# One block's k shift moved from TensorE to ScalarE, VectorE and DMA, with merged rotations, small statistics on ScalarE and a new plan

## The chip, the cores and the metric

The kernel runs on one core of a Trainium2 chip. The metric is the device time of one execution in microseconds. A run is an execution of one kernel; runs are taken in rounds together with runs of the kernel before on the same chip. A ratio is the mean time of one kernel's runs over that of the kernel before in the same rounds, so it isn't quite the ratio of the medians that are quoted; the bracket behind it is its 95% interval. Different jobs ran on different chips, so kernels of different jobs are compared through their ratios. 0.1% is 0.35 us.

## The reference

Two kinds of block alternate, twice each, over 2048 rows of 512 columns:

```python
def _A_ref(q, k, v, shift_k, ssm_k, ssm_D):
    # k_shift: causal sum of 4 taps along the rows, one set of taps per column
    for t in range(4):
        k_shift = k_shift + k_pad[:, t:t + S, :] * shift_k[:, 3 - t][None, None, :]
    kv = k_shift * v
    y  = (causal convolution of kv with ssm_k along the rows, by FFT)   # cut
    return q * (y + kv * ssm_D)

def _B_ref(x, w_gate, w_up, w_down):
    return (silu(x @ w_gate) * (x @ w_up)) @ w_down

x = A_q
for _ in range(2):                      # written out in the reference
    x = x + _A_ref(_layernorm(x), A_k, A_v, A_shift_k, A_ssm_k, A_ssm_D)
    x = x + _B_ref(_layernorm(x), B_w_gate, B_w_up, B_w_down)
```

The products kv don't depend on x, so the convolution is computed once and used by both layers.

## The kernel before

The rows are cut into four blocks of 512, and each block of each layer into two feed-forward units of 256 rows. So there are 16 units, run in the order layer 0 and then layer 1 of block 0, the same of block 1, and so on. TensorE works through the units; the convolution of the next blocks (transforms as matmuls, butterflies and products of spectra on VectorE) is laid between them.

In the profile PE is TensorE, PEld its weight loads, DVE VectorE, ACT ScalarE, POOL GpSimd and SP the engine that issues most DMAs. By the names in the program, z is a normalised row block, ptz and zT its transpose (by TensorE in the first unit, by DMA in all later ones), pf the gate and up matmuls, sg their silu, ht the copied up part and then its product with sg, pd the down projection, ps the transforms and the k shift, vt a block of v and then kv.

A planner decides what stands where. Each piece of work is entered with its engine, an estimate of its cost, the buffers that it reads and writes, and for a DMA the time `lat` from issue to landing. A list scheduler then fixes one order for each engine. Its tuning figures are constants at the head of the file:

```python
SLK = 8.59
ST1 = lambda l, c, h: (l, c, h) in {(0, 2, 0), (0, 3, 0), (1, 0, 1)}   # units whose first statistics go to ScalarE
K_ACT = lambda b: b in {3}            # blocks whose k shift does not use TensorE
T0, FLOOR = -8.68, -22.15
DUR = [21.8, 16.2, 25.01, ...]        # cut
STRETCH = {1: {"PE": 1.87, "DVE": 1.47, "ACT": 1.76, "POOL": 1.0, "SP": 341.8}, ...}   # cut
```

Within an engine the order is strict. An instruction that waits holds up all behind it, and a change of any cost or `lat` may give another order everywhere.

The k shift has two forms. With TensorE, four taps are four accumulating matmuls with diagonal matrices, 64 matmuls of 128 columns in a block:

```python
def shift_mul(b, ring, conv, after=(), due=None):
    for r in range(R):
        ...                            # 16 matmuls of 128 columns: kT (shifted by j rows) x dg[j], j = 0..3
        add("ACT", act(D), lambda ...: nc.scalar.copy(out=ks.t[:], in_=ps.t[:]), ...)
        dve(D, lambda ...: nc.vector.tensor_mul(out=vt[b].t[:, r, :], in0=ks.t[:], in1=vt[b].t[:, r, :]), ...)
```

Without TensorE, 16 ScalarE instructions multiply by a tap, three VectorE sums add the four, four DMA transposes turn the result, and two VectorE products multiply by v:

```python
def shift_mul_t(b):
    for j, (t, h) in ((3, (a, 0)), (2, (a, 1)), (1, (c, 0)), (0, (c, 1))):
        for dt in range(KD):
            add("ACT", 0.66, lambda ...: nc.scalar.activation(..., func=ACT.Copy, scale=tapF.t[:, dt, j:j + 1]), ...)
    for t, h in ((a, 1), (c, 0), (c, 1)):
        dve(4 * D, lambda ...: nc.vector.tensor_add(out=a.t[:, 0], in0=a.t[:, 0], in1=t.t[:, h]), ...)
    for r in range(R):
        add("SP", 1.25, lambda r=r: nc.sync.dma_start_transpose(out=ks.t[:, 0, r], in_=a.t[:, 0, r]), ..., lat=4.0)
    ...                                # two VectorE products of 1024 elements with v
```

The butterflies multiply by i, which swaps real and imaginary part, in four instructions of 512 elements:

```python
def rotated(m, i, j, dst, plus, minus, conv):
    for slot, part, op in ((plus, 0, ALU.subtract), (plus, 1, ALU.add), (minus, 0, ALU.add), (minus, 1, ALU.subtract)):
        dve(D, lambda ...: nc.vector.tensor_tensor(out=dst.t[:, slot, part], in0=m.t[:, i, part], in1=m.t[:, j, 1 - part], op=op), ...)
```

Of the kernel before, what the change touches and what calls it, by code (L numbers as in the profile page):

```python
# [9 lines left out]
P = 128  # L10
F32 = mybir.dt.float32
# [3 lines left out]
ALU = mybir.AluOpType  # L15
# [4 lines left out]
SLK = 8.59  # L20
H_DMA = lambda b: b in {2, 3}
ST1 = lambda l, c, h: (l, c, h) in {(0, 2, 0), (0, 3, 0), (1, 0, 1)}
ST2 = lambda l, c, h: (l, c, h) in {(0, 1, 0), (0, 1, 1), (1, 0, 0)}
ASL = 2.32
K_ACT = lambda b: b in {3}
# [3 lines left out]
HSL = 18.8  # L29
Z_ACT = lambda l, c, h: (l, c, h) in {(0, 1, 1), (0, 3, 0), (0, 3, 1), (1, 0, 0), (1, 0, 1), (1, 1, 1), (1, 2, 0), (1, 2, 1)}  # L30
N_ACT = lambda l, c, h: (l, c, h) in {(0, 3, 0), (0, 3, 1), (1, 1, 0), (1, 3, 0)}
Z_DMA = lambda i, j: False
D_DMA = lambda l, c, h: False
X_PE = lambda l, c, h: (l, c, h) in {(0, 1, 0), (0, 1, 1), (1, 3, 1)}
RINGS = {}
T0, FLOOR = -8.68, -22.15
DUR = [21.8, 16.2, 25.01, 22.43, 22.47, 23.48, 19.26, 20.4, 22.2, 24.98, 20.06, 26.08, 20.64, 23.98, 22.98, 26.0]
STRETCH = {1: {"PE": 1.87, "DVE": 1.47, "ACT": 1.76, "POOL": 1.0, "SP": 341.8},
           2: {"PE": 1.0, "DVE": 1.93, "ACT": 1.53, "POOL": 1.0, "SP": 1.62},
           3: {"PE": 1.55, "DVE": 1.54, "ACT": 2.16, "POOL": 1.0, "SP": 2.21}}  # L40
# [231 lines left out]
def kernel(  # L272
# [69 lines left out]
    ident, nhalf = whole("ident", [P, P]), whole("nhalf", [P, 1], F32)  # L342
    tapT, drow = whole("tapT", [P, KD, KS]), new("jk", "drow", [P, D])
# [198 lines left out]
    def rotated(m, i, j, dst, plus, minus, conv):  # L542

        for slot, part, op in ((plus, 0, ALU.subtract), (plus, 1, ALU.add), (minus, 0, ALU.add), (minus, 1, ALU.subtract)):
            dve(D, lambda slot=slot, part=part, op=op: nc.vector.tensor_tensor(
                out=dst.t[:, slot, part], in0=m.t[:, i, part], in1=m.t[:, j, 1 - part], op=op),
                [(m, key((i,), (part,))), (m, key((j,), (1 - part,)))], [(dst, key((slot,), (part,)))], conv=conv)
# [67 lines left out]
    def accumulate(z, sl, slots, part, t):  # L615
        add("POOL", 1.3, lambda: nc.gpsimd.dma_start(out=z.t[:, sl, part, :], in_=t.t[:], accum_op=ALU.add),
            r=[t, (z, key(slots, (part,)))], w=[(z, key(slots, (part,)))], lat=5.0, conv=True)

    def product(i, j, slots=range(4), conv=True):
# [22 lines left out]
        for part in (0, 1):  # L642
            zk = (z, key(slots, (part,)))
            if part and first and Z_DMA(i, j):
                dve(n * D, lambda: nc.vector.tensor_mul(out=z.t[:, sl, 1, :], in0=x.t[:, sl, 0, :], in1=g.t[:, sl, 1, :]),
                    [(x, key(slots, (0,))), (g, key(slots, (1,)))], [zk], conv=conv)
            else:
                t1 = new("t4", "t1", [P, n, D])
                dve(n * D, lambda t1=t1, part=part: nc.vector.tensor_mul(out=t1.t[:], in0=x.t[:, sl, 0, :],  # L649
                                                                         in1=g.t[:, sl, part, :]),  # L650
                    [(x, key(slots, (0,))), (g, key(slots, (part,)))], [t1], conv=conv)
                if part and Z_DMA(i, j):
                    accumulate(z, sl, slots, part, t1)
            t2 = new("t4", "t2", [P, n, D])
            dve(n * D, lambda t2=t2, part=part: nc.vector.tensor_mul(out=t2.t[:], in0=x.t[:, sl, 1, :],  # L655
                                                                     in1=g.t[:, sl, 1 - part, :]),
                [(x, key(slots, (1,))), (g, key(slots, (1 - part,)))], [t2], conv=conv)
            comb = ALU.subtract if part == 0 else ALU.add
            if part and Z_DMA(i, j):
                accumulate(z, sl, slots, part, t2)  # L660
            elif first:
                dve(n * D, lambda t1=t1, t2=t2, part=part, comb=comb: nc.vector.tensor_tensor(
                    out=z.t[:, sl, part, :], in0=t1.t[:], in1=t2.t[:], op=comb), [t1, t2], [zk], conv=conv)
            else:
                dve(n * D, lambda t1=t1, t2=t2, comb=comb: nc.vector.tensor_tensor(  # L665
                    out=t1.t[:], in0=t1.t[:], in1=t2.t[:], op=comb), [t2], [t1], conv=conv)
                if Z_DMA(i, j):
                    accumulate(z, sl, slots, part, t1)
                    continue
                dve(n * D, lambda t1=t1, part=part: nc.vector.tensor_add(  # L670
                    out=z.t[:, sl, part, :], in0=z.t[:, sl, part, :], in1=t1.t[:]), [t1], [zk], conv=conv)
# [57 lines left out]
    def ln_stats_act(c, rows, after=()):  # L729

        n = len(rows)
        mv, sm = new("mv", "mv", [P, n, 2], F32, parts=2 * n), new("st", "sm", [P, 2 * n], F32, parts=2 * n)
        for o, i in enumerate(rows):
            jk = new("jk", "jk", [P, D])
            add("ACT", 0.62, lambda jk=jk, o=o, i=i: nc.scalar.activation(
                out=jk.t[:], in_=xs[c].t[:, i, :], func=ACT.Copy, accum_out=sm.t[:, o:o + 1]), r=[(xs[c], (i,))], w=[jk, (sm, (o,))], after=after)
        nm = new("st", "nm", [P, n], F32)
        add("DVE", 0.08, lambda: nc.vector.tensor_scalar(out=nm.t[:], in0=sm.t[:, 0:n], scalar1=-1.0 / D, scalar2=None,
                                                         op0=ALU.mult), r=[(sm, range(n))], w=[nm])
        for o, i in enumerate(rows):  # L740
# [5 lines left out]
        add("DVE", 0.08, lambda: nc.vector.tensor_scalar(out=ve.t[:], in0=sm.t[:, n:2 * n], scalar1=1.0 / D, scalar2=LN_EPS,  # L746
                                                         op0=ALU.mult, op1=ALU.add), r=[(sm, range(n, 2 * n))], w=[ve])
        add("DVE", 0.08, lambda: nc.vector.tensor_scalar(out=mv.t[:, :, 0], in0=nm.t[:], scalar1=-1.0, scalar2=None,
                                                         op0=ALU.mult), r=[nm], w=[(mv, range(n))])
        add("POOL", PW, lambda: nc.gpsimd.tensor_tensor(out=rstd.t[:], in0=ve.t[:], in1=nhalf.t[:].to_broadcast((P, n)),  # L750
                                                          op=ALU.pow), r=[ve, nhalf], w=[rstd])
        return mv, rstd

    def shift_of(st, n, due=None):
        mv, rstd = st
        nmr = new("ve", "nmr", [P, n], F32)
        add("DVE", 0.08, lambda: nc.vector.scalar_tensor_tensor(out=nmr.t[:], in0=mv.t[:, :, 0], scalar=-1.0, in1=rstd.t[:],  # L757
                                                                op0=ALU.mult, op1=ALU.mult), r=[mv, rstd], w=[nmr], due=due)
        return nmr

    def normalise(dst, dkeys, view, c, i, o, st, nmr=None):
        mv, rstd = st
        if nmr is not None:
            add("ACT", 0.71, lambda: nc.scalar.activation(out=view(), in_=xs[c].t[:, i, :], func=ACT.Identity,  # L764
                                                            scale=rstd.t[:, o:o + 1], bias=nmr.t[:, o:o + 1]),
                r=[(xs[c], (i,)), nmr, rstd], w=[(dst, dkeys)])
            return
        return add("DVE", 0.325, lambda: nc.vector.tensor_scalar(out=view(), in0=xs[c].t[:, i, :], scalar1=mv.t[:, o, 0:1],
                                                          scalar2=rstd.t[:, o:o + 1], op0=ALU.subtract, op1=ALU.mult),
            r=[(xs[c], (i,)), mv, rstd], w=[(dst, dkeys)])  # L770
# [3 lines left out]
    def apply_norm(c, h, layer=0, on_act=False, after=(), due=None):  # L774
        rows = range(HP * h, HP * h + HP)
        st = ln_stats_act(c, rows, after) if on_act or ST1(layer, c, h) else ln_stats(c, rows)
# [6 lines left out]
    def prologue(layer, c, h, on_pe=False):  # L783
# [24 lines left out]
        for o, i in enumerate(rows):  # L808
# [8 lines left out]
            add("ACT", act(D), lambda pt=pt, o=o: nc.scalar.copy(out=zT.t[:, :, o, :], in_=pt.t[:]), r=[pt], w=[(zT, (o,))])  # L817
# [6 lines left out]
    def ffn(unit):  # L824
# [15 lines left out]
        groups = [range(f, min(f + 4, NF)) for f in range(0, NF, 4)]  # L840
        k = 0
        for fts in groups:
            n = len(fts)
            sg = new("sg", "sg", [P, n, W], parts=2)
            ht = new("ht", "ht", [P, n, W], parts=2)
# [50 lines left out]
        if xpe:  # L896
            for o in range(HP):
                i = HP * h + o
                add("ACT", act(D), lambda o=o, i=i: nc.scalar.copy(out=x.t[:, i, :], in_=pds[o].t[:]), r=[pds[o]], w=[(x, (i,))],
                    due=(unit, 1.0, 3.0, "h"))  # L900
        elif PD_ACT:
# [6 lines left out]
            if D_DMA(layer, c, h):  # L908
                add("POOL", 1.0, lambda: nc.gpsimd.dma_start(out=x.t[:, sl, :], in_=dn.t[:], accum_op=ALU.add),
                    r=[dn, (x, rows)], w=[(x, rows)], lat=4.0, due=(unit, 1.0, 4.0, "h"))  # L910
            else:
                dve(HP * D, lambda: nc.vector.tensor_add(out=x.t[:, sl, :], in0=x.t[:, sl, :], in1=dn.t[:]), [dn], [(x, rows)],  # L912
                    due=(unit, 1.0, 4.0, "h"))
# [10 lines left out]
    add("DVE", 0.07, lambda: nc.vector.memset(nhalf.t[:], -0.5), w=[nhalf])  # L924
    add("DVE", 0.2, lambda: nc.vector.memset(drow.t[:], 0.0), w=[drow], due=-69)
# [174 lines left out]
```

## Time and profile before

The median is 354.61 us (3 runs, 354.59 to 355.1); the profiled execution has a span of 353.0 us. The prediction shows this profile and reads it.

To read it: TensorE's stream is the floor. What the span has above it is the start, the end, and holes in which TensorE waits. VectorE is close to full in the first two thirds and half idle afterwards.

### The profile page before, as it was taken

What the parts mean: (1) busy time and instruction counts of PE and PEld (TensorE: products, weight loads), DVE (VectorE), ACT (ScalarE), POOL (GpSimd) and SP (SyncE); (2) the same over time, 40 slices, a digit from 0 to 9 for tenths busy, and PEclk for the clock granted to TensorE, in tenths of its full rate; (3) what the DMA queues carried; (4) which work ended last, traced back from release to release, by engine and by line L of the source; (5) the groups of instructions that cost most, each with busy time, mean ns of one, the idle gap of its engine ahead of it and who ended that gap; (6) DMA issues with size and microseconds to landing.
All of it is one profiled execution on the core that took longest, in us unless ns stands there. A gap on an engine that the chain in (4) does not pass through costs nothing.

```text
span 353.0 us, 6745 instructions
## 1 busy us (share of the span) xinstructions
PE 344.6 (98%) x2688; PEld 253.1 (72%) x2688; DVE 276.6 (78%) x511; ACT 248.4 (70%) x474; POOL 43.9 (12%) x45
## 2 busy tenths in 40 slices
PE   8998999989999999999999999999999999999996
PEld 6656777768688585858677686858586777777684
DVE  7976989998979999999999999999974333636120
ACT  6887984769789684728979993947597665646460
POOL 4100111102110311111112010111101000000000
PEclk9999999999999999999999999999999999999999
DMA  7999220020152321010411032010111010002000
GB/s 265 282 340 346 49 73 18 0 32 0 33 149 50 97 96 32 0 30 2 77 46 33 28 93 59 2 30 3 30 33 31 32 30 2 15 17 30 31 2 30
DMA packets 39897, 22.44 MB, mean 64 GB/s; under 512 B 31669, under 2 KB 37690, under 8 KB 39866
## 3 DMA queue, kind: packets, MB, share of 16 engines
q1 hardware_dynamic: 39194, 21.43, 23.5%
q10 hardware_dynamic: 672, 0.59, 0.5%
q8 instruction: 21, 0.34, 0.4%
q14 instruction: 10, 0.08, 0.1%
HBM read 12.33 MB, written 2.10 MB: 41 GB/s over the span
## 4 chain that ended last, share of the span: by engine, by line
PE 55%; DVE 31%; DMA 4%; ACT 3%; issue 3%; POOL 3%; DVEq 0%; POOLq 0%; ACTq 0%
PE pf L335 32%; PE pd L877 16%; DVE ht L864 4%; PE ps L335 4%; DMA vt<-in_A_v_dram 3%; DVE bnst L720 3%; DVE m L532 3%; DVE t L655 3%; DVE t L665 2%; DVE t L649 2%; PE ps L462 2%; DVE Z L670 2%; POOL rstd L725 2%; DVE n L790 1%; DMA zT<-z 1%
## 5 line engine op out<-in xcount | busy, mean ns | idle before, releaser
L335 PE MATMUL pf<-zT,wg_sb 128*128 128x256 bf16 x896 | 116.1, 273 | 2.7 <-ACT zT L817 1.3
L335 PE MATMUL pf<-zT,wu_sb 128*128 128x256 bf16 x896 | 116.1, 273 | 0.0
L335 PEld LDWEIGHTS <-wg_sb 128*128 128x128 bf16 x896 | 87.5, 98 | 20.5 <-issue 2.1
L877 PE MATMUL pd<-wd_sb,ht 128*128 128x512 bf16 (+1 forms) x462 | 100.8, 373 | 0.5 <-DVE ht L864 0.5
L335 PEld LDWEIGHTS <-wu_sb 128*128 128x128 bf16 x896 | 87.7, 98 | 11.3
L857 ACT ACTIVATE sg<-pf 128x512 bf16<-128x512 f32 x112 | 68.2, 609 | 17.9 <-PE pf L335 16.7
L877 PEld LDWEIGHTS <-ht 128*128 128x128 bf16 x462 | 45.1, 98 | 49.0 <-DVE ht L864 1.4
L861 ACT CAST ht<-pf 128x512 bf16<-128x512 f32 x112 | 66.4, 593 | 14.7 <-PE pf L335 13.8
L864 DVE TENSOR_TENSOR ht<-ht,sg 128x1024 bf16<-128x1024 bf16 x64 | 39.5, 618 | 23.7 <-ACT ht L861 23.5
L725 POOL TENSOR_TENSOR rstd<-ve,nhalf 128x2 f32<-128x2 f32 x24 | 28.6, 1192 | 194.9 <-DVE ve L723 179.5
L905 ACT CAST dn<-pd 128x512 bf16<-128x512 f32 x26 | 13.9, 589 | 36.9 <-PE pd L877 36.9
L720 DVE BATCH_NORM_STATS2 bnst<-xc 128x6 f32<-128x512 bf16 x48 | 31.1, 685 | 0.5
L912 DVE TENSOR_TENSOR xc<-xc,dn 128x1024 bf16<-128x1024 bf16 x13 | 8.9, 686 | 21.7 <-ACT dn L905 21.7
L649 DVE TENSOR_TENSOR t<-X,G 128x2048 bf16<-128x2048 bf16 x18 | 21.9, 1216 | 0.0
L655 DVE TENSOR_TENSOR t<-X,G 128x2048 bf16<-128x2048 bf16 x18 | 21.9, 1216 | 0.0
L750 POOL TENSOR_TENSOR rstd<-ve,nhalf 128x2 f32<-128x2 f32 x8 | 11.1, 1386 | 80.0 <-DVE ve L746 80.0
L423 ACT ACTIVATE X<-ps 128x512 bf16<-128x512 f32 x32 | 17.8, 608 | 4.3 <-PE ps L335 3.0
L764 ACT ACTIVATE z<-xc,nmr,rstd 128x512 bf16<-128x512 bf16 x16 | 12.1, 806 | 4.2 <-DVE nmr L757 4.2
L665 DVE TENSOR_TENSOR t<-t,t 128x2048 bf16<-128x2048 bf16 x12 | 14.6, 1220 | 0.2
L670 DVE TENSOR_TENSOR Z<-Z,t 128x2048 bf16<-128x2048 bf16 x12 | 14.6, 1219 | 0.0
L790 DVE TENSOR_TENSOR n<-n,Yk 128x1024 bf16<-128x1024 bf16 x15 | 10.4, 692 | 4.3 <-ACT n L764 3.7
L423 ACT ACTIVATE H<-ps 128x512 bf16<-128x512 f32 x24 | 13.5, 638 | 0.0
(100 smaller groups left out, 319.1 us busy)
## 6 DMA issues: line engine op xcount, KB each, us to landing
vt<-in_A_v_dram SPq DMA_DIRECT2D x4, 512.0 KB, 9.0
xc<-in_A_q_dram SPq DMA_DIRECT2D x4, 512.0 KB, 5.2
out_dram<-xc SPq DMA_DIRECT2D x15, 128.0 KB, 1.8
wg_sb<-in_B_w_gate_dram SPq DMA_DIRECT2D x1, 1792.0 KB, 12.9
wu_sb<-in_B_w_up_dram SPq DMA_DIRECT2D x1, 1792.0 KB, 7.4
wd_sb<-in_B_w_down_dram SPq DMA_DIRECT2D x1, 1792.0 KB, 12.5
hn<-in_A_ssm_k_dram SPq DMA_DIRECT2D x3, 512.0 KB, 6.8
hn<-in_A_ssm_k_dram ACTq DMA_DIRECT2D x1, 512.0 KB, 3.5
```

Source lines behind the costliest of these rows:

```text
L335: nc.tensor.matmul(o, lhsT=lhsT, rhs=rhs, start=(n == 0), stop=(n == len(terms) - 1))
L423: add("ACT", act(D), lambda: nc.scalar.activation(out=view(), in_=ps.t[:], func=ACT.Copy, scale=scale), r=[ps], w=[(buf, keys)], conv=conv)
L649: dve(n * D, lambda t1=t1, part=part: nc.vector.tensor_mul(out=t1.t[:], in0=x.t[:, sl, 0, :], in1=g.t[:, sl, part, :]), [(x, key(slots, (0 ...
L655: dve(n * D, lambda t2=t2, part=part: nc.vector.tensor_mul(out=t2.t[:], in0=x.t[:, sl, 1, :], in1=g.t[:, sl, 1 - part, :]), [(x, key(slots ...
L665: dve(n * D, lambda t1=t1, t2=t2, comb=comb: nc.vector.tensor_tensor(out=t1.t[:], in0=t1.t[:], in1=t2.t[:], op=comb), [t2], [t1], conv=conv)
L670: dve(n * D, lambda t1=t1, part=part: nc.vector.tensor_add(out=z.t[:, sl, part, :], in0=z.t[:, sl, part, :], in1=t1.t[:]), [t1], [zk], con ...
L720: add("DVE", 0.6, lambda st=st, i=i: nc.vector.bn_stats(out=st.t[:], in_=xs[c].t[:, i, :]), r=[(xs[c], (i,))], w=[st])
L725: add("POOL", PW, lambda: nc.gpsimd.tensor_tensor(out=rstd.t[:], in0=ve.t[:], in1=nhalf.t[:].to_broadcast((P, n)), op=ALU.pow), r=[ve, nha ...
L857: add("ACT", act(D), lambda ps=ps, o=o, sg=sg: nc.scalar.activation(out=sg.t[:, o:o + 2, :], in_=ps.t[:], func=ACT.Silu), r=[ps], w=[(sg, ...
L861: add("ACT", act(D), lambda ps=ps, o=o, ht=ht: nc.scalar.copy(out=ht.t[:, o:o + 2, :], in_=ps.t[:]), r=[ps], w=[(ht, (o // 2,))], due=(uni ...
L864: dve(n * W, lambda sg=sg, ht=ht: nc.vector.tensor_mul(out=ht.t[:], in0=ht.t[:], in1=sg.t[:]), [sg], [ht], due=(unit, k / pairs, 0.0, "h"))
L877: nc.tensor.matmul((pds[o] if not cs.start else pds[HP]).t[:, cs], lhsT=ht.t[:, q, o * P:(o + 1) * P], rhs=wt["d"].t[:, ft, cs], start=(ft ...
```

## The change

Its intent: take 64 matmuls of block 2 off TensorE, pay for them on ScalarE and VectorE, give VectorE some relief by merging instructions and moving small ones, and tune the plan anew. The core of the diff:

```diff
-K_ACT = lambda b: b in {3}
+K_ACT = lambda b: b in {2, 3}
-SLK = 8.59
+SLK = 25.89
 ...                       # likewise ST1, ST2, ASL, HSL, Z_ACT, N_ACT, X_PE, T0, FLOOR, DUR, STRETCH
 def rotated(m, i, j, dst, plus, minus, conv):
-    for slot, part, op in (... four of 512 ...):
+    def swapped(src, first, step):
+        return bass.AP(src.tensor, src.offset + first * D, [src.ap[0], [step * D, 2], [1, D]])
+    for op, re in ((ALU.subtract, plus), (ALU.add, minus)):
+        first, step = (2 * re, 2 * (plus + minus - 2 * re) + 1)
+        dve(2 * D, lambda ...: nc.vector.tensor_tensor(
+            out=swapped(dst.t[:], first, step), in0=m.t[:, i], in1=swapped(m.t[:], 2 * j + 1, -1), op=op), ...)
 ...
 def ln_stats_act(c, rows, after=(), key_=None):
-    add("DVE", 0.08, lambda: nc.vector.tensor_scalar(out=nm.t[:], in0=sm.t[:, 0:n], scalar1=-1.0 / D, ...))
+    add("ACT", TINY, lambda: nc.scalar.mul(out=nm.t[:], in_=sm.t[:, 0:n], mul=-1.0 / D), ...)
 ...                       # ve and the shift nmr = -mean * rstd likewise
-            add("ACT", act(D), lambda ...: nc.scalar.copy(out=zT.t[:, :, o, :], in_=pt.t[:]), ...)
+            add("ACT", act(D), lambda ...: nc.scalar.copy(out=zT.t[:, :, o, :], in_=pt.t[:]), ..., due=Z_DUE)
 ...
+                    # with the residual on TensorE, the eviction also sums: its row sum is not computed again
+                    add("ACT", act(D) + 0.12, lambda ...: nc.scalar.activation(
+                        out=x.t[:, i, :], in_=pds[o].t[:], func=ACT.Copy, accum_out=sm.t[:, o:o + 1]), ...)
```

The rest of the diff carries these pieces through (a buffer for epsilon, the mean kept negative) or takes out code that no setting used.

## The prediction

> **What bounds the kernel now.** I read the page's first part and its chain first, then the waits of TensorE, then busy time by stretches, then the groups by form.
>
> The page's head and busy shares:
> ```profile
> span 353.0 us, 6745 instructions
> PE 344.6 (98%) x2688; PEld 253.1 (72%) x2688; DVE 276.6 (78%) x511; ACT 248.4 (70%) x474; POOL 43.9 (12%) x45
> ```
> A busy share of 98% doesn't say by itself that TensorE is full, since the durations of overlapping matmuls are modelled. The spacing of matmuls says it. These pieces of the chain that ended last (start, length, what) are unbroken runs:
> ```profile
> 1.72 2.63 PE wm L1066 x23
> 8.84 3.57 PE ps L335 x64
> ...
> 21.08 11.77 DMA vt<-in_A_v_dram
> 32.97 0.44 DVE vt L513
> 33.97 1.09 ACT zT L817 x2
> ...
> 312.52 12.23 PE pf L335 x112
> 324.75 6.04 PE pd L877 x28
> ```
> 12.23 / 112 = 0.1092 us for a 256-wide matmul, 6.04 / 28 = 0.2157 for a 512-wide one, 3.57 / 64 = 0.0558 for a 128-wide one; the 23 warm-up matmuls ran cold, 0.114 each. The groups by form count 1822 of 256 columns (1792 gate and up, 28 down, 2 identity), 591 of 512 (434 down, 152 transforms, 5 identity), 248 of 128 (192 k shift, 56 transposes). Sum: 199.0 + 127.5 + 13.8, plus 2.6 warm-up and 0.2 for the taps = 343.1 us. Add 1.7 before the first matmul and 3.9 after the last piece of down projection (that chain leaves TensorE at 349.1): 348.7 of 353.0. So TensorE's own stream is the bound, with only some 4.3 us of holes. The waits of TensorE (total, times, longest) name nearly all of them:
> ```profile
> PE pf L335 <- ACT zT L817: 1.3, 1, 1.3
> PE pf L335 <- DMA zT<-z: 1.0, 1, 1.0
> PE pd L877 <- DVE ht L864: 0.5, 1, 0.5
> PE pf L335 <- ACT sg L857: 0.4, 1, 0.4
> ```
> The 1.3 is the start of the first feed-forward unit at 35.1 us (a unit is 256 rows; there are 16). In the chain above, v's second block lands at 32.85, only then can VectorE multiply it, free a slot for ScalarE's copy of the shifted k, and only then does ScalarE copy the first transposed z.
>
> VectorE is the second bound, in the first two thirds alone. Busy time by stretches (length, then PE, PEld, DVE, ACT, POOL):
> ```profile
> 34.00:238.00 204.00, 201.05 (x1533) 147.15 (x1533) 194.43 (x329) 154.82 (x304) 29.33 (x20) 1.00 0.20 45
> 238.00:353.00 115.00, 111.53 (x863) 84.14 (x860) 56.16 (x118) 67.58 (x121) 8.58 (x10) 1.00 0.10 22
> ```
> 95% of VectorE is used up to 238 us, 49% after. That is why the chain runs through VectorE between 98 and 235 us although TensorE hardly stops there: the plan balanced the two. Shortening TensorE's stream there gains only what VectorE and ScalarE can follow.
>
> **What the Trainium skill says.** "TensorE: Matmul & The Clock Gate", section "Wait — 56ns, not 53.3ns?", gives warm start-to-start times of 55.6 and 215.7 ns for 128 and 512 columns and 106.7 for a cold 128: the trace agrees (55.8, 215.7, 114). "Perfetto Trace Analysis", "Identifying the Most-Contended Engine", warns that matmul busy time is a poor measure; hence the spacing above. "ScalarE: Activation LUTs", "What ACT_TABLE_LOAD costs", gives an ACTIVATE as 186 ns + 0.833 per element, about 93 more for a per-partition pointer and 93 less by overlap: 706 ns for 512 elements with a pointer scale. The trace's tap multiplies have means of 772 and 785 and follow each other at 0.66. For two elements it gives about 190; the trace has 203 for a one-element ACTIVATE. "Vector Engine (DVE) Microarchitecture Reference", "5.1 Performance modes — why throughput varies by op and dtype", asks two-byte data with an innermost step of 1 or -1 for the doubled rate, and says how the engine streams an operand with a negative step was not measured. The merged rotations step backwards in an outer dimension only, so I expect the full rate; no trace here shows it yet.
>
> **The change part by part.** The counts are from comparing the two programs' instruction orders engine by engine.
>
> TensorE: block 2's shift was 64 matmuls of 128 columns, 64 x 0.0558 = 3.57 us, gone. One more warm-up matmul, +0.11. All others are the same in number (the units that add the residual on TensorE are two and the last, as before, only others). Net -3.46 us. This is the one certain gain, since nearly every microsecond of TensorE's stream counts.
>
> These groups (busy, mean) carry the rest:
> ```profile
> L592 ACT ACTIVATE ka<-kTb,tapF 128x512 bf16<-128x512 bf16 x8 | 5.4, 772 | 0.0
> L596 DVE TENSOR_TENSOR ka<-ka,kc 128x2048 bf16<-128x2048 bf16 x2 | 2.4, 1222 | 0.1
> L545 DVE TENSOR_TENSOR Z<-m 128x512 bf16<-128x512 bf16 x12 | 4.5, 416 | 0.0
> L538 DVE TENSOR_TENSOR Z<-m 128x1024 bf16<-128x1024 bf16 x6 | 4.0, 688 | 0.1
> L738 DVE TENSOR_SCALAR nm<-sm 128x2 f32<-128x2 f32 x8 | 1.3, 162 | 1.6 <-ACT jk L735 1.5
> ```
> VectorE, at the rates at which back-to-back instructions follow each other in the trace (0.335 us for 512 two-source elements, 0.60 for 1024, 1.136 for 2048, 0.32 for a 512 normalise, about 0.08 for a two-element one). Added: three 2048 sums 3.4, two 1024 products 1.2, two more normalises net 0.65: +5.25. Removed: four 512 products 1.35; 36 rotations of 512 (12.1) become 18 of 1024 (10.8), 1.3; 24 small statistics 1.9 and six shifts 0.5. Net about +0.2: no relief by throughput. By mean durations, the small ones at 0.16 and the rotations at 0.416 against 0.688, it would be -3.2. The truth for the critical engine is nearer the first, plus the in-order waits that go with the small ones: in the groups VectorE idled 1.6 us before nm and 2.4 before nmr.
>
> ScalarE: 16 more tap multiplies x 0.66 = 10.6; 26 small ones x 0.2 = 5.2; minus four shifted-k copies (1.9), two sums fused into the eviction (1.2) and two normalises net (1.4): about +11.3 on 248.4. It has 49 us idle between 34 and 238, so it should hold on average. It sits tight only in unit 0, where the same order shows unit 1's normalise now on ScalarE ahead of unit 0's last evictions.
>
> SyncE: four more transposes, their sources ready long before unit loads behind them in the queue; a z transpose lands in 2.4 us. Hidden.
>
> First z: in the new order VectorE multiplies the two shifted k rows before it writes z, so both wait for v at 32.9 us. z comes at about 33.9, TensorE turns it, ScalarE copies at about 34.1 to 35.1. I expect the first unit at 35.1 to 35.5 as before, so I credit nothing for "first z first"; the hole before it shrinks by about 0.4 because the new order puts two more inverse matmuls ahead of it, which is inside the -3.46.
>
> Later holes: I summed the rates along each engine's order up to each unit's z, and compared with TensorE's sum to that unit's start. The distance TensorE minus VectorE is 18.6 us before and 15.6 after at unit 4; 18.9 and 22.8 at unit 6; 25.9 and 25.4 at unit 8. At unit 4 it falls 3 us; before, z was there 5.3 us ahead, and about 3.7 is the least that any unit had. So unit 4 may lose up to 1.4 us, less the waits VectorE no longer has. For ScalarE in unit 0 the distance from last eviction to its down projection falls from 9.4 to 6.9, where ScalarE's accumulated lag is 10.6 against an offset of 3.9: nearly nothing left, so a hole of 0.5 to 1.5 around unit 0 and 1. Against that, three holes (1.0 for a late transpose at 77 us, 0.4, 0.5) belong to the old order; a new plan made for this balance should lose about half of them. I book -1.5 and +1.2.
>
> Sum: 354.6 - 3.5 - 1.5 + 1.2 = 350.8 us.
>
> **Rivals.** First, VectorE becomes the bound: it gets no lighter while TensorE's stream shrinks 3.5 us. For it: 95% busy up to 238 us. Against it: the freed waits (about 3 us), and that the new order pushes VectorE's work later (the sum at unit 9's last product is 203.6 against 210.7), into the part where it is half idle. If it holds, time stays at 353 to 355. Second, ScalarE holds up the evictions because 11 us more run on it, unit 0 and 1 losing 2 to 3 us and others some: 352 to 354. Third, the new plan closes all late holes: 343.1 - 3.5 of work plus the fixed 5.6 and the 1.3 at the start gives a span of 346.5, some 348 in time. Even that is just short of 2% (347.5). Fourth, the reversed step drops the rotations to half rate, 18 x 0.53 = 9.6 us more on VectorE: about 360. I give that 3%.
>
> **Range and chances.** 348.6 to 353.2 covers the plan being good (only the starting hole left, and half a microsecond) up to the first two rivals in part. More than 2% faster needs more than every late hole gone: 4%. More than 2% slower (over 361.7) needs the half rate or a badly ordered queue: 3%.
>
> **What would show it.** Right: the shift's 128-wide group at x128 instead of x192, matmul spacing unchanged, first unit at 35.1 to 35.5, TensorE's named waits between 1.5 and 4 us, VectorE's merged rotations at about 0.69. Wrong: rotations near 1.2 us; a wait of TensorE on a z transpose or ht of over 2 us; a first unit before 34.5 us, which would make "first z first" a gain that I denied; or ScalarE's evictions named before TensorE in unit 0 to 1.

## The result

The changed kernel takes 351.19 us (median of 4 runs, 351.0 to 353.21); the kernel before, in the same rounds, 354.73 (4 runs, 354.59 to 355.1). The ratio is 0.9913 [0.9888, 0.9938]: 0.9% less by the means, which is 3.1 us, and 3.5 us by the medians. It counts as the same at 2%. The mean holds one run of 353.21 us, with a granted clock of 0.994; the other three have 0.998 to 1.000 and take 351.0 to 351.24.

The head and the busy shares of the changed kernel's profile:

```profile
span 349.4 us, 6596 instructions
PE 341.3 (98%) x2597; PEld 249.7 (71%) x2625; DVE 276.7 (79%) x466; ACT 258.9 (74%) x508; POOL 38.1 (11%) x46
```

The span fell by 3.6 us, as the time did. VectorE has 45 instructions fewer and the same busy time, 276.7 against 276.6. ScalarE has 10.5 us more. The trace lacks 28 of the 2625 matmuls (the weight loads are all there), so counts of matmuls are taken from the program's order below.

Busy time by stretches (length, then PE, PEld, DVE, ACT, POOL, the granted clock, the DMA share, GB/s):

```profile
34.00:238.00 204.00, 202.83 (x1531) 149.14 (x1547) 195.33 (x306) 162.55 (x315) 25.00 (x21) 1.00 0.21 49
238.00:350.00 112.00, 107.66 (x819) 80.43 (x824) 56.89 (x103) 69.82 (x140) 7.04 (x10) 0.99 0.09 22
```

VectorE is as full up to 238 us as before (96%), and TensorE is fuller there, 202.83 against 201.05. The relief of VectorE didn't come, and TensorE got its gain without it.

The groups that carry the change (busy, mean ns of one, idle before):

```profile
L334 PE MATMUL ps<-dg,kTb 128*128 128x128 bf16 x128 | 8.0, 219 | 0.0
L549 DVE TENSOR_TENSOR Z<-m 128x1024 bf16<-128x1024 bf16 x6 | 3.9, 683 | 0.0
L600 DVE TENSOR_TENSOR ka<-ka,kc 128x2048 bf16<-128x2048 bf16 x4 | 4.9, 1217 | 0.0
L752 ACT ACTIVATE nmr<-nm,rstd 128x1 f32<-128x1 f32 x10 | 2.6, 310 | 0.0
L738 ACT ACTIVATE ve<-sm,eps 128x2 f32<-128x2 f32 x8 | 2.4, 296 | 0.3
```

and of before, the shift on TensorE:

```profile
L335 PE MATMUL ps<-dg,kTb 128*128 128x128 bf16 x192 | 12.0, 219 | 0.0
```

x192 became x128. The mean of 219 ns is not the cost of one; the spacing is (0.0558 us). The merged rotation of 1024 elements takes 683 ns, which is what a plain 1024 takes. The small instructions on ScalarE take 0.3 us where they have a pointer operand.

The spacing is unchanged. From the chain that ended last (start, length, what), 12.23 us for 112 matmuls, as before:

```profile
1.45 6.03 DMA kn<-in_A_k_dram
...
36.87 1.91 PE pf L334 x16
...
58.11 12.23 PE pf L334 x112
```

The chain also shows the start, which is later than before: the first unit begins at 36.87, where before it was 35.1. The shares of the engines in the chain, first of the kernel before and then of the changed one:

```profile
PE 55%; DVE 31%; DMA 4%; ACT 3%; issue 3%; POOL 3%; DVEq 0%; POOLq 0%; ACTq 0%
```

```profile
PE 80%; DVE 14%; ACT 2%; DMA 2%; issue 1%; SPq 0%; DVEq 0%
```

TensorE carries 80% of the chain instead of 55%, and the waits of TensorE name only two of over 0.2 us (total, times, longest), both before 8 us:

```profile
PE wm L1068 <- POOL ident masks.py:199: 1.7, 1, 1.7
PE pt L378 <- DMA kn<-in_A_k_dram: 1.1, 1, 1.1
```

The waits on z transposes, on ht and on sg that the prediction shows of before are gone.

**Where the 3.6 us came from.** I summed TensorE's stream (count of each width times its spacing, as in the prediction) up to the start of each unit, and took it from the time at which the unit starts in the trace. The difference is what TensorE has lost by then:

| unit | before: start | stream | lost | after: start | stream | lost |
|---|---|---|---|---|---|---|
| 0 | 35.1 | 31.2 | 3.9 | 36.9 | 31.6 | 5.3 |
| 4 | 120.7 | 115.6 | 5.1 | 110.4 | 104.9 | 5.5 |
| 8 | 198.7 | 193.0 | 5.7 | 191.3 | 185.7 | 5.6 |
| 12 | 275.0 | 268.7 | 6.3 | 272.3 | 266.1 | 6.2 |
| 15 | 330.6 | 324.4 | 6.2 | 327.1 | 320.9 | 6.2 |

At the last unit the changed kernel is 3.5 us ahead, and its stream is 3.5 us shorter (324.4 - 320.9). What is lost is 6.2 us in both, but in different places. The kernel before lost 3.9 up to the first unit and 2.3 later; the changed one loses 5.3 up to the first unit and 0.9 later. The start took 1.4 us and the better plan gave 1.4 us back. (Between units the two plans lay other work, so the starts of unit 4 are not comparable, only what is lost.)

**Why the first unit is late.** VectorE's timeline (start, length, line, operation, count, idle before it and what ended that), before:

```profile
29.85 0.73 DVE L768 TENSOR_SCALAR z<-xc,mv,rstd 128x512 bf16<-128x512 bf16 x2 [0.81 <-POOL rstd L725]
32.97 0.76 DVE L513 TENSOR_TENSOR vt<-ks,vt 128x512 bf16<-128x512 bf16 x2 [2.39 <-DMA vt<-in_A_v_dram]
```

and after:

```profile
33.44 0.76 DVE L513 TENSOR_TENSOR vt<-ks,vt 128x512 bf16<-128x512 bf16 x2 [0.89 <-DMA vt<-in_A_v_dram]
34.12 0.73 DVE L764 TENSOR_SCALAR z<-xc,mv,rstd 128x512 bf16<-128x512 bf16 x2
```

The new plan puts the two products that need v's second block ahead of z. z is needed for the first unit, and v lands only at 33.3. The planner enters v with a `lat` of 4.5 us; from issue to landing it took 8.9 us in this execution, 11.8 in that of before and 11.4 in that of a1_same below. So the planner counted on the products to be done much earlier. In this execution another thing was late too: the first block of k landed 6.0 us after its issue, so TensorE stood 1.1 us and then worked off a backlog. Which of the two sets the start is tested below.

### The profile page after: what moved, and what is told of

Its sections match the earlier page's. It is cut to its first block, busy times and chain, and to the rows that moved or that the text cites. A ratio compares the mean times of both kernels' runs of the same rounds, so it can differ in the third digit from the quotient of the medians.

```text
span 349.4 us, 6596 instructions
## 1 busy us (share of the span) xinstructions
PE 341.3 (98%) x2597; PEld 249.7 (71%) x2625; DVE 276.7 (79%) x466; ACT 258.9 (74%) x508; POOL 38.1 (11%) x46
## 4 chain that ended last, share of the span: by engine, by line
PE 80%; DVE 14%; ACT 2%; DMA 2%; issue 1%; SPq 0%; DVEq 0%
PE pf L334 46%; PE pd L874 23%; PE ps L334 7%; PE ps L462 2%; PE ps L697 2%; DMA kn<-in_A_k_dram 2%; DVE ht L861 2%; DVE bnst L709 1%; DVE t L649 1%; DVE t L657 1%; DVE t L645 1%; DVE Z L659 1%; DVE ka L600 1%; DVE Z L654 1%; DVE m L532 1%
## 5 line engine op out<-in xcount | busy, mean ns | idle before, releaser
L874 PE MATMUL pd<-wd_sb,ht 128*128 128x512 bf16 (+1 forms) x445 | 97.8, 372 | 1.1
L861 DVE TENSOR_TENSOR ht<-ht,sg 128x1024 bf16<-128x1024 bf16 (+1 forms) x64 | 39.3, 618 | 24.8 <-ACT ht L858 24.8
L714 POOL TENSOR_TENSOR rstd<-ve,nhalf 128x2 f32<-128x2 f32 x24 | 26.2, 1092 | 215.8 <-DVE ve L712 206.6
L740 POOL TENSOR_TENSOR rstd<-ve,nhalf 128x2 f32<-128x2 f32 x8 | 7.7, 960 | 63.9 <-ACT ve L738 63.9
L334 PE MATMUL ps<-hs,fwd 128*128 128x512 bf16 x39 | 12.1, 404 | 0.2 <-issue 0.2
## 6 DMA issues: line engine op xcount, KB each, us to landing
wg_sb<-in_B_w_gate_dram SPq DMA_DIRECT2D x1, 1792.0 KB, 11.8
```

What stands on the lines that cost most here:

```text
L334: nc.tensor.matmul(o, lhsT=lhsT, rhs=rhs, start=(n == 0), stop=(n == len(terms) - 1))
L714: add("POOL", PW, lambda: nc.gpsimd.tensor_tensor(out=rstd.t[:], in0=ve.t[:], in1=nhalf.t[:].to_broadcast((P, n)), op=ALU.pow), r=[ve, nha ...
L861: dve(n * W, lambda sg=sg, ht=ht: nc.vector.tensor_mul(out=ht.t[:], in0=ht.t[:], in1=sg.t[:]), [sg], [ht], due=(unit, k / pairs, 0.0, "h"))
L874: nc.tensor.matmul((pds[o] if not cs.start else pds[HP]).t[:, cs], lhsT=ht.t[:, q, o * P:(o + 1) * P], rhs=wt["d"].t[:, ft, cs], start=(ft ...
```

## The experiments

Twelve kernels ran; all gave right results. I group them by the question that they answer. The theory: the gain is TensorE's shorter stream in full, the plan keeps VectorE and ScalarE just out of its way, and the start was lost to z behind v. The rivals: the start was lost to k; TensorE's saving is partly hidden and other parts of the change made the gain; VectorE is the bound.

**The granted clock, for all that follows.** All runs fall into two groups. In a1_same three runs with a granted clock of 0.998 to 1.000 take 351.1 to 351.6 us, and three with 0.994 or 0.995 take 353.3 to 353.9. The ratios and medians below mix the groups. What can stand behind a lower clock is seen in five profiles: stretches in which TensorE had half the clock, of 3.41 us (two each in a2_k2_on_pe and a4_rot4, one each in a6_norm_dve and b1_k2_only) or 6.83 (a3_old_plan). Of a4_rot4, first a wait of TensorE and then such a stretch (length, then PE, PEld, DVE, ACT, POOL, the granted clock, the DMA share, GB/s):

```profile
256.00:259.70 3.70, 0.04 (x1) 0.00 (x0) 3.63 (x4) 3.34 (x8) 0.15 (x1) 1.00 0.39 86
260.50:263.90 3.40, 3.40 (x18) 2.43 (x17) 3.37 (x6) 2.18 (x5) 0.00 (x0) 0.50 0.00 0
```

In the traces each of the five waits of TensorE of 3.2 us or more has one that begins within 1 us of its end; of nine waits of 2.0 to 3.0 us two have one. At half clock 3.41 us cost TensorE about 1.7 us of work (an estimate, half of it). So a long wait is dearer than its length. The other profiles have none between 10.4 us and their last 2 us. Whether the slower runs of a1_same have one after their wait at the first unit isn't shown, since only a run at 0.998 was traced; a5_kn_late_plan, a7_v_late_plan and a8_both, whose waits there are at most 1.3 us, have no run below 0.999 in 18.

### What set the start: k, or z behind v?

**a1_same.** No edit: a fresh profile.

> The changed kernel again, unedited, to see whether the late landing of k's first block (7.5 us after the start, against 5.8 in the kernel before) comes back. If it was chance: k lands near 5.8, no cold matmuls after it, the first feed-forward unit starts at 35.1 to 35.5 and the time is about 349.6. If it belongs to this kernel: k lands near 7.5 again, the first unit starts near 36.9 and the time is 351.0 to 351.3.

Measured: 352.43 us (6 runs, 351.11 to 353.92), ratio 0.9917 [0.9879, 0.9954], span 349.3. k landed 4.3 us after its issue this time, and TensorE didn't stand there; yet the first unit started at 36.7. The chain from v's issue (start, length, what):

```profile
21.95 11.43 DMA vt<-in_A_v_dram
...
33.50 0.76 DVE vt L513 x2
34.26 0.34 DVE z L764
...
34.64 0.72 PE ptz L811 x8
...
36.90 1.75 PE pf L334 x16
```

and TensorE's first wait:

```profile
PE ptz L811 <- DVE z L764: 2.0, 1, 2.0
```

So the ratio repeats. k's lateness was chance (in the other 13 of the 14 traces k takes 3.9 to 4.5 us), and it cost nothing: it only filled the time in which TensorE would have waited for z.

**a5_kn_late_plan.** The planner is told that the first k is slow, so that it puts other work ahead. (The new plan also has five more warm-up matmuls.)

```diff
-... nc.sync.dma_start(out=kn[b].t[:], in_=k_t[:, b]), w=[kn[b]], lat=3.9, due=due)
+... nc.sync.dma_start(out=kn[b].t[:], in_=k_t[:, b]), w=[kn[b]], lat=5.6, due=due)
```

> Only the planner's figure for the landing of k's first block is raised from 3.9 to 5.6 us, so that eight transform matmuls stand ahead of k's transposes. Theory that TensorE's wait for k and the cold clock after it cost the changed kernel 1.7 us at the start: the first unit starts at 35.1 to 35.6, the time is 349.3 to 349.9. Rival, that the start is set by v's landing and the wait for k is hidden: the first unit starts at 36.5 to 37 and the time stays at 351.

Measured: 351.7 us (350.73 to 352.1), ratio 0.9892 [0.9858, 0.9925], on the same chip as a1_same. The first unit starts at 37.0. The interval overlaps that of a1_same, and the start didn't move: k is not what sets it.

**a7_v_late_plan.** The planner is told how slow v's second block is.

```diff
-... in_=v_t[:, b]), w=[vt[b]], lat=4.5 if b else 5.3, due=due, after=after)
+... in_=v_t[:, b]), w=[vt[b]], lat=11.4 if b == 1 else 4.5 if b else 5.3, due=due, after=after)
```

> The changed kernel; only the planner's figure for the landing of v's second block is raised from 4.5 to 11.4 us, what both traces show. That puts the first z ahead of the shift products on VectorE and ahead of the shifted k copies on ScalarE. Theory that the wait for v ahead of the first z is what keeps the first feed-forward unit at 36.7 us and that TensorE's stream carries an earlier start to the end: first unit at 32.8 to 33.5, TensorE's wait for z gone, time 347.5 to 349 (3 us less than the changed kernel). Rival, that VectorE and ScalarE set the pace behind it: the same early start, but holes before units 1 to 5, time 350.5 to 352.

The 11.4 us is what a1_same shows; in the changed kernel's profile v took 8.9, so not both traces show it. Measured: 350.49 us (350.23 to 351.05) against 355.6 of before, ratio 0.9848 [0.9824, 0.9872], span 348.8. This is the fastest kernel. On VectorE z now stands ahead of the products:

```profile
30.63 0.74 DVE L764 TENSOR_SCALAR z<-xc,mv,rstd 128x512 bf16<-128x512 bf16 x2 [0.81 <-POOL rstd L714]
```

and the first unit starts at 33.7, 3.0 us earlier than in a1_same. That shows z behind v to be what set the start. But the 3.0 us do not last, and the time is that of the rival (350.5 to 352), not of the theory (347.5 to 349): unit 1 starts 2.4 us earlier than in the profile of the changed kernel (55.5 against 57.9), unit 5 only 0.6 (128.1 against 128.7), and the last 0.6 (326.5 against 327.1). TensorE's waits show where some of it went:

```profile
PE pf L334 <- DMA zT<-z: 0.5, 1, 0.5
PE pf L334 <- ACT ht L858: 0.5, 1, 0.5
PE pf L334 <- ACT sg L854: 0.4, 1, 0.4
```

Starting earlier, TensorE catches up with ScalarE and VectorE, which didn't become faster. By ratio the kernel is 0.7% (2.4 us) below a1_same; but half the runs of a1_same had a clock of 0.994 or 0.995, and none here. Over runs of 0.998 and more alone the ratios are 0.9859 and 0.9900, 1.5 us apart; the two also ran on different chips, and the profiled spans differ by 0.5. So it beats the kernel before by 1.5%, measured on one chip, and the changed kernel by something between 0.5 and 1.5 us at the same clock.

**a8_both.** Both `lat` edits together.

> The previous kernel with the raised figure for k's first landing as well. If the start is set by z once v no longer is: equal to the previous kernel within 0.4 us. If k's landing matters in some executions: narrower spread, median up to 0.5 us lower.

Measured: 352.26 us (351.29 to 353.11), ratio 0.9894 [0.9869, 0.9919]; span 351.3, first unit at 35.4. I had expected it to equal a7_v_late_plan and missed: it is 1.8 us slower in the median, on the same chip. An edit that is right by itself gave another order everywhere, with the first unit later. This was the first sign that a change of the planner's input tests more than what was meant.

### Does TensorE's shorter stream count in full?

**c1_pe_plus64.** 64 idle matmuls of 128 columns are put back on TensorE before the transforms of block 2, inside pieces of work that the planner already has, with their cost unchanged. The orders of the other engines stay as they are.

```diff
+    def extra(ps, ev):
+        for _ in range(8 if ev.name == "X2" else 0):
+            nc.tensor.matmul(ps.t[:, 0:P], lhsT=ident.t[:], rhs=ident.t[:], start=True, stop=True)
 ...
-    lambda ps=ps, f=f, r=r: mm(ps.t[:], [(fT(f, r), rows.t[:, r, :])]),
+    lambda ps=ps, f=f, r=r: [extra(ps, ev), mm(ps.t[:], [(fT(f, r), rows.t[:, r, :])])],
```

> The changed kernel with 64 idle matmuls of 128 columns (identity times identity, overwritten by what follows) ahead of the third block's forward transforms, where the removed shift stood; the orders of VectorE and ScalarE are checked to be unchanged instruction for instruction. It puts back 3.57 us of TensorE's stream and nothing else. TensorE theory: 3.3 to 3.8 us slower than the changed kernel, about equal to the kernel before (ratio to it 0.998 to 1.004). If VectorE paced the kernel there: under 1.5 us slower.

Measured: 356.17 us (355.82 to 356.9) against 354.63, ratio 1.0037 [1.0005, 1.0069]; span 354.5. The added group, and the largest later wait:

```profile
L521 PE MATMUL ps<-ident 128*128 128x128 bf16 x64 | 4.9, 219 | 0.0
```

```profile
PE ps L334 <- DMA hs<-hr: 1.5, 1, 1.5
```

Against a1_same the ratio is 1.2% higher, about 4.3 us, and the profiled span 5.2 us longer; the matmuls are 64 x 0.0558 = 3.57 us. The unit in which they lie takes 29.6 us instead of 26.0, 3.6 more, and nothing is recovered later; unit 7, with the wait shown, takes 20.0 instead of 18.3, which adds to the 3.3 to 3.8 expected. So the stream counts in full. With the 64 matmuls back, the changed kernel has no gain left over the one before.

**a2_k2_on_pe.** The changed kernel with `K_ACT` back at `{3}`, planned anew with the new figures.

```diff
-K_ACT = lambda b: b in {2, 3}
+K_ACT = lambda b: b in {3}
```

> The changed kernel with the third block's shift back on TensorE, all plan figures kept. TensorE's stream is 3.5 us longer, VectorE's 3.3 us shorter and its distance to TensorE 0.6 to 16 us larger. TensorE theory: 3 to 4 us slower than the changed kernel, about equal to the kernel before. VectorE theory: no slower than the changed kernel.

Measured: 362.32 us (360.76 to 364.42), ratio 1.0185 [1.015, 1.022]; span 362.3. That is some 9.6 us above the changed kernel where I expected 3 to 4. TensorE waits 4.1 us on z transposes and has two stretches of half clock, about 3.4 us of work; a third of the loss is the matmuls, the rest is an order that doesn't fit and what follows from its waits. c1_pe_plus64 changes the stream and no order.

### Is VectorE the bound, and did its relief matter?

**c2_dve_plus3.** Three products of 2048 elements are each done twice, again with the planned orders unchanged.

```diff
-    dve(n * D, lambda t1=t1, part=part: nc.vector.tensor_mul(out=t1.t[:], ...),
+    dve(n * D, lambda t1=t1, part=part: [nc.vector.tensor_mul(out=t1.t[:], ...)
+        for _ in range(2 if (i, j, part) in {(0, 2, 0), (0, 2, 1), (2, 0, 0)} else 1)],
```

> The changed kernel with three products of 2048 elements on VectorE issued twice (same result), at the same plan and with TensorE's and ScalarE's orders unchanged: 3.4 us more of VectorE between about 100 and 150 us, what the three tap sums cost. If VectorE is a second bound with no room left up to unit 10: 2 to 3.5 us slower than the changed kernel, seen as TensorE waiting for z or ht in units 6 to 10. If VectorE had room there: under 1 us.

Measured: 353.64 us (352.25 to 354.49), ratio 0.9959 [0.9925, 0.9992]; span 351.2. The added work is 3 x 1.136 = 3.4 us. The ratio is 0.4% above a1_same, about 1.5 us. In the profile, 0.7 us of the longer span was there before the edit, at the first unit (v landed 0.7 us later than in a1_same, and z with it; 37.4), and two later units lose 1.3 together, with one new wait:

```profile
PE ps L334 <- DVE Z L538: 0.6, 1, 0.6
```

So neither pure theory holds. VectorE has about half of 3.4 us in hand in that stretch. It stands close behind TensorE without being the bound.

**a4_rot4.** The four rotations of 512 elements back, planned anew (the body of `rotated` as before).

> The changed kernel with the four separate rotations of 512 elements in place of the two of 1024; TensorE's work is unchanged. Theory that TensorE's stream alone sets the time, with VectorE close behind: VectorE gains 1.2 us of work by throughput, its distance to TensorE shrinks by about 1 us in most units, the time rises by 0 to 0.7 us. Rival, that VectorE is the bound: it rises by 1.2 us or more. If the merged ones ran at half rate, this kernel would be faster.

Measured: 361.04 us (360.32 to 361.87), ratio 1.0158 [1.0119, 1.0197]: about 8.6 us above a1_same, and both expectations missed. VectorE has 1.2 us more busy time, which can't be it. The order is. In the changed kernel, near 240 us, the sum that completes a unit's x (the line of xc) stands before the butterflies (the line of m is their first step):

```profile
239.57 0.69 DVE L787 TENSOR_TENSOR xc<-xc,n 128x1024 bf16<-128x1024 bf16 x1
240.18 2.35 DVE L532 TENSOR_TENSOR m<-X 128x2048 bf16<-128x2048 bf16 x2
```

In a4_rot4 it stands behind them:

```profile
243.00 2.35 DVE L532 TENSOR_TENSOR m<-X 128x2048 bf16<-128x2048 bf16 x2
...
247.94 0.68 DVE L783 TENSOR_TENSOR xc<-xc,n 128x1024 bf16<-128x1024 bf16 x1
```

x is what the statistics, z and the next unit wait for. Units 10 and 11 take 24.4 and 20.8 us where they take 20.1 and 20.0 in the changed kernel, and TensorE waits 3.7 us at a stretch for a z transpose. The rest is in part clock: the wait at the first unit is 2.0 us as in a1_same, but half clock followed it, and the unit starts at 38.8 instead of 36.7.

**a9_rot4_same_plan.** The same question without a new plan: each planned rotation issues its two instructions of 512 elements in place.

```diff
+        def both(op, re):
+            for part in (0, 1):
+                slot = re if part == 0 else plus + minus - re
+                nc.vector.tensor_tensor(out=dst.t[:, slot, part], in0=m.t[:, i, part], in1=m.t[:, j, 1 - part], op=op)
 ...
-            dve(2 * D, lambda ...: nc.vector.tensor_tensor(out=swapped(...), in0=m.t[:, i], in1=swapped(...), op=op), ...)
+            dve(2 * D, lambda op=op, re=re: both(op, re), ...)
```

> The changed kernel with the same plan and order, but each merged rotation issued as two of 512 elements inside the same planned step. In the earlier run with four rotations the planner also moved other instructions, and the time rose by 9 us. If the reordering did that: now 0 to 1 us above the changed kernel, with VectorE's work 1.2 us larger. If VectorE's throughput did it: again 4 us or more above.

Measured: 353.81 us (352.98 to 355.35), ratio 0.9941 [0.9915, 0.9968]; span 352.1. That is 0.24% above a1_same, about 0.9 us, on another chip and so not certain. One of the groups:

```profile
L550 DVE TENSOR_TENSOR Z<-m 128x512 bf16<-128x512 bf16 x12 | 4.4, 418 | 0.0
```

By what follows back to back, 18 pairs of 0.335 against 18 of 0.60 are 1.3 us. How much of that reaches the time isn't shown. The profile's span is 2.8 us longer than a1_same's, but for two other reasons: v landed 0.8 us later, and one rstd on GpSimd took 3.64 us where a1_same has 0.69, for which ScalarE stood 1.8 us and then TensorE 1.6 in unit 0:

```profile
43.38 3.64 POOL L743 TENSOR_TENSOR rstd<-ve,nhalf 128x2 f32<-128x2 f32 x1 [12.62 <-ACT ve L741]
```

From unit 1 to the last, TensorE takes 0.1 us more than in a1_same in all, so the later rotations are hidden. What the merging is worth lies within the noise of these runs (the intervals of the two ratios overlap), and of a4_rot4's 8.6 us nearly all was the order, with the waits and the half clock that it brought.

**a6_norm_dve.** The small statistics (nm, ve and nmr) back on VectorE, planned anew. nmr is one product of two elements, since the mean is kept negative.

```diff
-        add("ACT", TINY, lambda: nc.scalar.mul(out=nm.t[:], in_=sm.t[:, 0:n], mul=-1.0 / D), ...)
+        add("DVE", 0.08, lambda: nc.vector.tensor_scalar(out=nm.t[:], in0=sm.t[:, 0:n], scalar1=-1.0 / D, ..., op0=ALU.mult), ...)
 ...                                   # ve likewise
-            for o in range(n):
-                add("ACT", TINY, lambda o=o: nc.scalar.mul(out=nmr.t[:, o:o + 1], ...), ...)
+            add("DVE", 0.08, lambda: nc.vector.tensor_tensor(out=nmr.t[:], in0=mean.t[:], in1=rstd.t[:], op=ALU.mult), ...)
```

> The changed kernel with the small statistics (negated mean, variance plus epsilon, shift) back on VectorE, everything else kept. TensorE's work is unchanged, VectorE gains 2.8 us by throughput and its distance to TensorE shrinks by 1 to 2.5 us. TensorE theory: the time rises by 0.3 to 1.5 us, seen as named waits of TensorE on ht or z. VectorE theory: by 2.8 us or more. If the small ones had been no burden: no change.

Measured: 358.6 us (358.0 to 359.31), ratio 1.0089 [1.0058, 1.012]: about 6 us above a1_same. TensorE waits 5.7 us on z transposes, 4.1 of it at once before unit 11, with half clock after it, and in the trace the same butterflies stand ahead of the same x as in a4_rot4. So what the small instructions cost on VectorE can't be told from this run. It stays open.

### What the new plan carries

**b1_k2_only.** The kernel before with the one line changed that moves block 2's shift.

```diff
-K_ACT = lambda b: b in {3}
+K_ACT = lambda b: b in {2, 3}
```

> The kernel before with the third block's shift by ScalarE, VectorE and transposes, and nothing else of the change, its old plan figures kept. TensorE's stream falls by 3.5 us to 339.6, VectorE's work rises by 3.3. In the new order VectorE's distance to TensorE in units 0 to 3 falls to 1 to 4 us, from 8 to 14. If the plan must be refitted for the gain to arrive: several holes, time 356 to 362. If removing TensorE's work suffices: 351.

Measured: 364.12 us (4 runs, 362.59 to 364.48) against 355.11, ratio 1.0232 [1.0198, 1.0266]; span 360.8. Moving the shift alone makes the kernel 2.3% slower (the interval reaches just under 2%; I expected 356 to 362 us), although TensorE's stream is 3.57 us shorter. Units 0 to 2 take 24.8, 24.0 and 21.8 us; in the kernel before 20.9, 21.2 and 20.9. The largest wait is in unit 0, with half clock behind it (the z that is named directly follows, on VectorE, the ht that the down projection reads):

```profile
PE pd L877 <- DVE z L768: 3.8, 1, 3.8
```

**a3_old_plan.** The changed kernel, all its code, with the plan figures and unit sets of before.

```diff
-SLK = 25.89
+SLK = 8.59
 ...                       # ST1, ST2, ASL, HSL, Z_ACT, N_ACT, X_PE, T0, FLOOR, DUR, STRETCH as before
```

> The changed kernel with all its parts but the plan figures and the choice of units of the kernel before. TensorE's and VectorE's work are those of the changed kernel; the distances in units 0 to 3 are 2 to 5 us. If the replanning carries the gain: 354 to 361. If the parts carry it: 351 to 352.5.

Measured: 365.48 us (364.1 to 366.05), ratio 1.0266 [1.0227, 1.0305], on the same chip as b1_k2_only; span 364.2. I expected 354 to 361. TensorE's largest wait:

```profile
PE pd L876 <- DVE ht L863: 4.4, 3, 3.5
```

Units 0 to 2 take 24.8, 25.0 and 21.8 us. The wait of 3.5 us lies in unit 0. There VectorE runs the butterflies, a sum of x, statistics and a sum of products of the convolution ahead of the ht that TensorE needs; in the kernel before ht stands between the butterflies. Of a3_old_plan:

```profile
48.97 2.35 DVE L534 TENSOR_TENSOR m<-X 128x2048 bf16<-128x2048 bf16 x2
...
57.25 0.68 DVE L863 TENSOR_TENSOR ht<-ht,sg 128x1024 bf16<-128x1024 bf16 x1
```

The shift's own sums aren't what stands in the way there: the first comes at 111.7, in unit 3. The step from here to the changed kernel is the figures and sets alone, and it is 3.5%, some 12 us, of which half clock for 6.83 us is about 3.4. Whether the figures (order) or the sets (which engine does which unit's statistics and normalising) carry it was not separated. The code makes a shorter stream possible; only the new figures and sets turn it into time.

## Why the prediction was right or wrong

The time (350.8 predicted, 351.19 measured) and the class are right, and the range held. Two terms of the sum were wrong by 1.1 and 1.4 us with opposite signs; that the sum came out within 0.4 us is in part luck.

**TensorE's stream, -3.46: right.** The group went from x192 to x128, the spacing is unchanged, the stream ahead of the last unit is 3.5 us shorter, and c1_pe_plus64 shows that 3.57 us put back cost 3.6 us in the unit where they lie, and some more by waits. One reading was off without harm: the warm-up matmuls start 0.107 us apart in the trace, not 0.114, since 2.63 us holds the tail of the last one; that is under 0.2 us of the sum.

**VectorE, no relief by throughput: right.** 0.2 us net was predicted; busy time went from 276.6 to 276.7. By mean durations it would have been -3.2, and the durations added up did fall by 3.3 us (306.1 to 302.8). But they overlap, and the time in which VectorE was busy didn't change; so the first way to count is the right one here. The merged rotations ran at the full rate (682 to 684 ns; 0.69 was predicted), so the fourth rival fell.

**ScalarE, +11.3: right in sum (+10.5 in busy time), wrong in a part.** The 26 small instructions were entered at 0.2 us; they take 0.207 (nm), 0.296 (ve) and 0.310 (nmr). By busy time they are 1.7 + 2.4 + 2.6 = 6.7 us instead of 5.2.

**"First z", credit nothing: wrong in size.** The step that failed is "z comes at about 33.9, TensorE turns it, ScalarE copies at about 34.1 to 35.1". It took v's landing from the trace of before (32.85; it was 33.4), let z follow the first product when both stand ahead of it (the two z end at 34.9), and let TensorE start the unit as soon as z was copied, although the new order puts 16 shift matmuls and three inverse ones before it. Measured, the first unit is at 36.7 to 36.9 where 35.1 to 35.5 was predicted, and what TensorE has lost by then is 5.3 us instead of 3.9. The mechanism, z behind v, was right, and a7_v_late_plan shows it. It also shows that being earlier at the start is worth little at the end.

**Later holes, -1.5 + 1.2 = -0.3: wrong in size.** The +1.2 was a hole of ScalarE in units 0 and 1 and one before unit 4. Neither came: the changed kernel's trace names no wait there, and what is lost goes from 5.3 at unit 0 to 5.5 at unit 4. At unit 4, where z was to lose 3 us of its lead, it was written 4.4 us ahead of the unit's start, against 5.3 before. The -1.5 was about right: the later losses went from 2.3 to 0.9 us, -1.4. So the distances along the engines' orders that I summed said "nearly nothing left", and there was enough. One reason is in the measurements: with the first unit 1.4 us later, ScalarE and VectorE get as much time in hand. a7_v_late_plan takes that time away, and there TensorE does wait for sg and ht. That the same happened by way of unit 0 in the changed kernel is argued from this, not shown by a run of its own.

**The rivals.** VectorE as the bound: in part (c2_dve_plus3 shows half of 3.4 us hidden). ScalarE holding up the evictions: not in the changed kernel, for a short time in a7_v_late_plan. All late holes closed: nearly so (0.9 left), and the later start took it back, which the third rival hadn't counted.

Two things that the prediction didn't foresee. It treated the new plan as a small correction; b1_k2_only and a3_old_plan show that it decides between 2.3 to 2.7% slower and 0.9% faster. And it expected nothing of the planner's belief about v, which is where the fastest version comes from.

## What to carry to other kernels

Here work taken off the engine that is the bound counted in full once the plan was made anew for the new balance; the same edit under the old figures cost more than it saved. Where an engine's own stream is the bound, try the two together. To measure one part of a scheduled kernel, keep the orders and change only what is issued at one place: the experiments that let the planner start again measured its reordering, 6 to 9 us, and not the part. And compare what a planner assumes of a DMA with the trace: one landing time that was 4 to 8 us off put the first unit's input behind a load that it didn't need.

## What the Trainium skill lacked or had wrong

- "Vector Engine (DVE) Microarchitecture Reference", "5.1 Performance modes — why throughput varies by op and dtype", leaves negative steps unmeasured. Here an outer step backwards, with runs of 512 two-byte elements forwards inside, costs nothing: 682 to 684 ns for 1024 elements with two sources, against 684 to 687 ns for the plain ones of the same butterflies.
- "TensorE: Matmul & The Clock Gate", "Back-to-back issue gap", gives 81 ns for 128 columns and 131 ns for 512 as the sustained spacing of pairs of weight load and matmul. In these traces, with a weight load for each matmul, the spacing is 55.8 ns and 215.7 ns over runs of 64 and 28.
- "ScalarE: Activation LUTs", "What ACT_TABLE_LOAD costs": its 186 ns plus about 93 for a pointer operand is some 6 to 11% low for the small instructions (188 by the page and 207 measured without a pointer, about 280 and 296 to 310 with one). I had used the figure without a pointer for all of them.
- No page that I read has how much a load's landing varies between executions: the first block of k landed 4.3 us after its issue in one and 6.0 us in another, and v's second block took 8.9 to 12.4 us beside the other loads where the plan assumed 4.5.
